# First attention of a four-layer kernel: mask pattern through TensorE, opening in another order, a fourth o_t, early residual loads, shared last norms

## The chip, the cores and the metric

The kernel runs on one core of a Trainium2 chip. A core has TensorE (PE, with its weight loads listed as PEld), VectorE (DVE), ScalarE (ACT), GpSimd (POOL) and SyncE (SP), and 16 DMA engines that SP, ACT and POOL feed from queues of their own. Each engine executes its instructions in order, and an instruction that waits holds those behind it. The metric is the device time of one execution in microseconds; the time before is the median of three runs. Times inside an execution count from the start of the profiled span. "L402" is line 402 of the kernel before.

## The reference, cut to what matters

The input x has 2048 rows of 576 columns. Four layers follow each other, each with a residual: attention (A), gated MLP (B), A, B.

```python
def A(x):                                   # 32 heads of 18
    q, k, v = split(x @ wqkv)
    idx = pos[:, None] - 2 * arange(8)      # 8 keys, two rows apart
    logits = where(idx >= 0, q . k[idx] * 18 ** -0.5, -1e9)
    return (softmax(logits) . v[idx]) @ wo
def B(x):
    z = gelu(x @ w_in)                      # 576 -> 4608
    z1, z2 = z[:, :2304], layernorm(z[:, 2304:])
    return (z1 * (w_sp @ z2 + b_sp)) @ w_out
x = x + A(layernorm(x)); x = x + B(layernorm(x)); x = x + A(layernorm(x)); x = x + B(layernorm(x))
```

## The kernel before, in words

The rows are held with even rows first and odd rows behind (`rows_of`), so that the eight keys of a row are neighbours. `layer_A` works on 17 query tiles of 120 rows (the first 128) with 128 keys each; a step is half a tile, that is 16 heads, so there are 34 steps (`NST`). An attention has an opening, the steps, and a tail.

**Row norms of the first layer.** `S_` takes the statistics of a row tile on DVE, `R_` the inverse root (an addition on DVE, a power on POOL), `A_` writes the normalised tile to one of four buffers `xn_bufs` on DVE. Tiles 0 to 3 are transposed into `xnT` by PE (`T_pe`, ScalarE copies), tiles 4 to 15 by DMA transposes on SP (`T_`, L266). The x tiles come in DMAs of one to four tiles. Before the norms PE runs 46 warm-up products of the identity (L626), and DVE fills unused weight rows with zeros (`zero_right`).

**Projections.** `VW(t, hh, dve)` makes half of v for tile t (five matmuls, `pv`) and evicts it into `v_ext` on DVE or ScalarE (L402, L404). `PG(d, qk, cc, dve)` makes 128 columns (block d of 0 to 4) of q or k for 512 rows (`pp`), evicts them into a staging tile `stg`, and when the staging tile has all its parts it issues DMAs that move each head to its place in `QK` (32 partitions a head; L78 on the queues it is given). Staging tiles are three of 1024 columns and, in the first layer, two pieces lent from the place of the gMLP weights `win2a`. (d, first half) for d of 3 and 4, and (4, each block of the second half), use the lent ones.

**The mask.** A head takes 18 of the 32 partitions that it has in `QK`. The 14 others hold a periodic pattern, so that the logits' matmul itself adds a large negative number outside the window. `build_window_rows` builds one period on POOL and DVE in `R`, writes it to DRAM (`win_period`, three DMAs on POOL's queue) and `load_pat` reads it back into the 14 rows of each quarter of `pat` (four DMAs on SP). `fill_window_rows(QK, half)` then copies the pattern over half of `QK` on DVE (L198); as it writes all partitions, the moves of q and k must come after it.

**Order of the opening.** All engines' orders are those of the program text (`manual_schedule`). After tiles 4 to 7 the text loads the pattern, normalises 8 to 11, fills half 0 of `QK`, takes the statistics of 12 to 15, and issues the PGs of columns 0 to 1023 in `order`, with R_ and A_ of 12 to 15 after the sixth entry and their transposes on SP after the last. Then come the v of tiles 4 to 7 (each first half evicted on DVE) and the first six PGs of the second half (`pre`, the first four evicted on DVE), with the first logits after two of them and the fill of half 1 after four.

**The steps.** Each step issues the logits of the next step (`L_mm`, L473), their exponentials on ScalarE (L482), and `PV`: 16 products with v (`O_ps`, L496), a reciprocal (L502), and the scaled result into `o_t` on DVE (L504). o_t buffers go round three; a full one is transposed by DMA on SP into `oT`, a ring of six tiles of 128 rows, directly (L511) or through `o_slot` (L515) and a DVE copy (`O_CP`, L524). The dictionary `table` then adds work by step number with `at(s, f, ...)`: the remaining PGs in steps 0 to 11 in the order of the list `pgs`, v, the output product `WO` (`pw`, L557) with its addition of the residual `xo` (L560), the load `XO` of two residual tiles at a time into three buffers, the store `XST`, and the next layer's row norm: `LN_STATS`, then `LN_AGGR` and `LN_POW` inside the next `PV`, then `LN_XN` on POOL (L259). `XN_ST` and `LN_T` store normalised rows to DRAM and read them back transposed for the gMLP.

**The tail.** Row tiles 12 to 15 (`tail_rows`) are normalised after the last step: two tiles' statistics, their roots, their POOL norms, then the same for the other two. `layer_B` begins with groups of eight units (`p1_group`, L907) whose results ScalarE evicts into row buffers `zp` (three); DVE and POOL normalise a finished row into `Z` (L971 to L980), which frees its buffer.

Of the kernel before, what the change touches and what calls it, by code (L numbers as in the profile page):

```python
# [63 lines left out]
class K:  # L64
# [50 lines left out]
    def build_window_rows(self, c, R):  # L115

# [5 lines left out]
        n = c.tile([P, 3], i32, name="win_n")  # L126
        g = c.tile([P, 3], i32, name="win_g")
        bits = c.tile([P, 5, 3], i32, name="win_bits")
        vf = c.tile([P, 5, 3], f32, name="win_vf")
        uu = c.tile([P, 4, 2], f32, name="win_uu")  # L130
        R0 = c.tile([P, 2, MR, 8], bf16, name="win_first")
        half = WB / 2
        nc.gpsimd.iota(n[:], pattern=[[1, 3]], base=15, channel_multiplier=1)
        nc.gpsimd.memset(R[:, 0, 0:8], half)
        nc.gpsimd.affine_select(out=R[:, 0, 0:8], in_=R[:, 0, 0:8], compare_op=ALU.is_ge, fill=-half,
                                base=0, pattern=[[1, 8], [0, 2], [-1, 8]], channel_multiplier=0)
        nc.gpsimd.memset(R[:, 1, 0:8], 0.0)
        nc.gpsimd.affine_select(out=R[:, 1, 0:8], in_=R[:, 1, 0:8], compare_op=ALU.not_equal, fill=-1.0,
                                base=-1, pattern=[[-1, 8], [0, 2], [1, 8]], channel_multiplier=0)
        nc.gpsimd.memset(R[:, 1, 7, :, 0:1], 1.0)  # L140
        for a, v in ((0, half), (1, 1.0)):
            nc.gpsimd.memset(R[:, a, 12, 0, :], v)
            nc.gpsimd.memset(R[:, a, 12, 1, :], -v)
        nc.gpsimd.memset(R[:, 0, 13], -2.5 * WB)
        nc.gpsimd.memset(R[:, 1, 13], 1.0)
        one = self.dram.tile([2, MR, 2 * P + 8], bf16, name="win_period")
        for xb in self.xn_bufs:
            nc.gpsimd.memset(xb[:, D:640], 0.0)

        def part0():  # L150
            nc.vector.tensor_scalar(out=n[:], in0=n[:], scalar1=15, scalar2=None, op0=ALU.bitwise_and)
            nc.vector.tensor_scalar(out=g[:], in0=n[:], scalar1=1, scalar2=None, op0=ALU.logical_shift_right)
            nc.vector.tensor_tensor(out=g[:], in0=g[:], in1=n[:], op=ALU.bitwise_xor)
            for i in range(4):
                nc.vector.tensor_scalar(out=bits[:, i, :], in0=g[:], scalar1=i, scalar2=1,
                                        op0=ALU.logical_shift_right, op1=ALU.bitwise_and)
            nc.vector.tensor_scalar(out=bits[:, 4, :], in0=n[:], scalar1=1, scalar2=None, op0=ALU.bitwise_and)

        def pads():
            nc.gpsimd.memset(pat[:], 0.0)  # L160

        def part1(eng):
            nc.vector.tensor_scalar(out=vf[:], in0=bits[:], scalar1=-2.0, scalar2=1.0, op0=ALU.mult, op1=ALU.add)
            Rf = R[:].rearrange("p a r b m -> p a r (b m)")
            nc.vector.tensor_scalar_mul(out=Rf[:, :, 0:8, :], in0=Rf[:, :, 0:8, :], scalar1=vf[:, 4, 1:2])
            nc.vector.tensor_tensor(out=uu[:], in0=vf[:, 0:4, 0:2], in1=vf[:, 0:4, 1:3], op=ALU.add)
            nc.vector.tensor_scalar_mul(out=Rf[:, 0, 8:12, :], in0=vf[:, 0:4, 1:2].to_broadcast([P, 4, 16]), scalar1=half)
            nc.vector.tensor_scalar_mul(out=Rf[:, 1, 8:12, :], in0=uu[:, :, 1:2].to_broadcast([P, 4, 16]), scalar1=0.5)
            for b_ in range(2):
                nc.vector.tensor_scalar_mul(out=R[:, 1, 8:12, b_, 0:1], in0=uu[:, :, 0:1], scalar1=0.5)  # L170
            for b_ in range(2):
                self.dma(one[:, :, b_ * P:(b_ + 1) * P].rearrange("a r (p m) -> p (a r) m", m=8),
                         R[0:16, :, :, b_, :].rearrange("p a r m -> p (a r) m"), eng=eng)

        def part2(eng):
            nc.gpsimd.tensor_copy(out=R0[0:1], in_=R[0:1, :, :, 0, :])
            nc.gpsimd.tensor_copy(out=R0[0:1, 1, 8:12, 0:1], in_=R[0:1, 1, 8:12, 0, 1:2])
            nc.gpsimd.memset(R0[0:1, 0, 11, :], 1.5 * WB)
            nc.gpsimd.memset(R0[0:1, 0, 13, :], -3.5 * WB)
            self.dma(one[:, :, 2 * P:2 * P + 8].rearrange("a r m -> (a r) m")[None, :, :], R0[0:1].rearrange("p a r m -> p (a r) m"), eng=eng)  # L180

        def load(eng):
            for j in range(4):
                self.dma(pat[32 * j + DH:32 * j + 32, :, :], one[:].rearrange("a r x -> r a x"), eng=eng)
        self.load_pat = load
        return part0, pads, part1, part2
# [42 lines left out]
    def ln_stats(self, pool, x_t, nrows, want_nmr=True, eps_eng=None):  # L229
        nc = self.nc  # L230
        eps_eng = eps_eng or nc.vector
        st = pool.tile([P, 2, nc.vector.BN_STATS_DIM], f32, name="ln_st", tag="ln_st", bufs=3)
        for s in range(2):
            nc.vector.bn_stats(out=st[:nrows, s, :], in_=x_t[:nrows, s * 288:(s + 1) * 288])
        mv = pool.tile([P, 2], f32, name="ln_mv", tag="ln_mv", bufs=3)
        nc.vector.bn_aggr(out=mv[:nrows, :], in_=st[:nrows, :, :])
        rstd = pool.tile([P, 1], f32, name="ln_rstd", tag="ln_rstd", bufs=3)
# [979 lines left out]
```

## Time and profile before

| what | value |
|---|---|
| median of 3 runs | 1168.77 us (1164.8 to 1170.26) |
| the profiled execution's own time | 1172.01 us |
| its span | 1170.2 us |
| PE, DVE, ACT, POOL busy | 98%, 47%, 29%, 24% of the span |
| first attention, to the first gMLP matmul | 126.39 us |
| first steps: output product of step 0 | 51.08 us |
| last step's output product | 120.64 us |
| mean granted TensorE clock | 0.997 |

A line of a timeline has the start, the duration of a group of like instructions, engine, line, operation, the output and input names, shapes and count; in brackets the idle time of the engine just before, and what ended it. A line of the chain of waits has start, duration, engine or DMA, name, line. A line of the windows has the stretch, its length, then for PE, PEld, DVE, ACT and POOL the busy time and number of instructions, then the granted PE clock (1.00 is full), the DMA engines' busy share and GB/s. Matmul ends are modelled and overlap by some 0.15 us.

### The profile page before, as it was taken

To read this page: it belongs to the slowest core of one execution; us is meant where nothing else is said; L and a number is where in the kernel's file an instruction comes from. 1 tells how busy PE (TensorE), PEld (TensorE's weight loads), DVE (VectorE), ACT (ScalarE), POOL (GpSimd) and SP (SyncE) were. 2 spreads that over 40 slices of the span, in tenths; PEclk is the share of its full clock that TensorE was granted. 3 is DMA by queue.
4 is the path that set the end of the run, shared out by engine and by line. 5 is a ranking of instruction groups with operands and counts; after the bars stand their busy time and mean duration, and the time that the engine had idled before them with its cause. 6 is when DMAs were issued, how large, how long until landed. Compare 5 with 4: busy or idle time off the path is not lost.

```text
span 1170.2 us, 19968 instructions
## 1 busy us (share of the span) xinstructions
PE 1150.5 (98%) x8163; PEld 612.5 (52%) x8258; DVE 550.0 (47%) x1167; ACT 338.8 (29%) x493; POOL 278.8 (24%) x389
## 2 busy tenths in 40 slices
PE   9999999999999999999999999999999999999998
PEld 5457544444444444457755774444444444444677
DVE  8668598322333332244555886963322223322321
ACT  5589455111100111101247884541011110111000
POOL 4659865000000000001153786640000000000000
PEclk9999999999999999999999999999999999999999
DMA  9599697000000000049646997930000000001332
GB/s 217 119 160 294 193 212 142 23 12 12 12 1 12 12 12 1 6 138 296 169 107 105 204 256 182 242 91 1 12 12 12 12 12 1 12 1 46 111 105 74
DMA packets 183240, 106.45 MB, mean 91 GB/s; under 512 B 135225, under 2 KB 164441, under 8 KB 183149
## 3 DMA queue, kind: packets, MB, share of 16 engines
q1 hardware_dynamic: 170285, 84.85, 31.6%
q0 software_dynamic: 6512, 14.57, 4.8%
q10 hardware_dynamic: 6352, 5.75, 1.6%
q8 instruction: 64, 1.05, 0.4%
q14 instruction: 27, 0.22, 0.1%
HBM read 42.40 MB, written 21.77 MB: 55 GB/s over the span
## 4 chain that ended last, share of the span: by engine, by line
PE 85%; POOL 7%; DMA 3%; DVE 2%; issue 2%; ACT 0%; SPq 0%; POOLq 0%; DVEq 0%; ACTq 0%
PE pg L1055 42%; PE po L1104 12%; PE pz L1031 6%; PE pz1s L1031 6%; PE pzs L907 5%; PE pp L436 4%; PE pz L907 4%; POOL ln_xn L259 4%; PE pv L410 2%; PE O_ps L496 1%; PE pw L557 1%; PE L_ps L473 1%; POOL ln_rstd L582 1%; DMA QK<-stg 1%; DMA o_slot<-o_t 1%
## 5 line engine op out<-in xcount | busy, mean ns | idle before, releaser
L1055 PE MATMUL pg<-Wq,Z 128*128 128x512 bf16 x2260 | 497.9, 379 | 2.5
L1055 PEld LDWEIGHTS <-Z 128*128 128x128 bf16 x2304 | 225.5, 98 | 271.8
L1059 DVE TENSOR_TENSOR g_tmp<-pg,ln_xn 128x512 f32<-128x512 f32 x144 | 99.6, 692 | 421.5 <-PE pg L1055 419.5
L1050 ACT ACTIVATE z1T<-pz 128x1024 bf16<-128x1024 f32 x36 | 34.9, 1021 | 500.8 <-PE pz L1031 500.8
L78 POOL DMA_DIRECT2D wout<-in_B_w_out_dram x4 | 4.3, 1070 | 598.8 <-PE pg L1055 598.8
L1104 PE MATMUL po<-wout,Z 128*128 128x288 bf16 x1152 | 141.4, 286 | 0.0
L482 ACT ACTIVATE P_sb<-L_ps 128x1440 bf16<-128x1440 f32 (+3 forms) x136 | 125.1, 972 | 21.1 <-PE L_ps L473 19.7
L1104 PEld LDWEIGHTS <-Z 128*128 128x128 bf16 x1152 | 112.7, 98 | 28.8
L907 PEld LDWEIGHTS <-xnT 128*128 128x128 bf16 (+1 forms) x800 | 68.7, 98 | 80.0 <-issue 15.5
L1060 DVE TENSOR_TENSOR Z<-g_tmp,z1T 128x512 bf16<-128x512 f32 x144 | 99.7, 692 | 12.2
L956 DVE BATCH_NORM_STATS2 z_st<-zp 128x6 f32<-128x512 bf16 (+1 forms) x160 | 91.0, 617 | 5.1 <-ACT zp L954 4.8
L1031 PEld LDWEIGHTS <-w 128*128 128x128 bf16 (+1 forms) x640 | 53.7, 97 | 74.0 <-issue 13.6
L436 PE MATMUL pp<-xnT,wqk_sb 128*128 128x512 bf16 x341 | 82.2, 382 | 2.5 <-DVE o_t L504 1.3
L259 POOL TENSOR_SCALAR ln_xn<-x_new,ln_mv,ln_rstd 128x576 bf16<-128x576 f32 x32 | 73.3, 2291 | 2.6
L1114 DVE TENSOR_TENSOR x_new<-po,xo 128x288 f32<-128x288 f32 (+1 forms) x64 | 28.8, 455 | 87.4 <-PE po L1104 83.9
L1031 PE MATMUL pz<-xnT,w 128*128 128x512 bf16 (+1 forms) x316 | 66.3, 380 | 0.2
L1031 PE MATMUL pz1s<-xnT,w 128*128 128x512 bf16 (+1 forms) x310 | 64.9, 379 | 0.9 <-issue 0.8
L78 POOL DMA_DIRECT2D QK<-stg x81 | 49.5, 614 | 46.0 <-DVE oT L524 14.8
L907 PE MATMUL pzs<-win2a,xnT 128*128 128x512 bf16 (+1 forms) x235 | 59.9, 364 | 0.4 <-issue 0.3
L907 PE MATMUL pz<-win2a,xnT 128*128 128x512 bf16 (+1 forms) x233 | 58.3, 357 | 0.6 <-issue 0.2
L980 POOL TENSOR_SCALAR Z<-zp,z_mv,z_rstd 128x256 bf16<-128x256 bf16 x32 | 55.7, 1740 | 3.4
L436 PEld LDWEIGHTS <-wqk_sb 128*128 128x128 bf16 x360 | 33.5, 98 | 38.3 <-DVE o_t L504 1.5
(113 smaller groups left out, 936.6 us busy)
## 6 DMA issues: line engine op xcount, KB each, us to landing
xres<-x_new SPq DMA_DIRECT2D x48, 288.0 KB
xo<-xres SPq DMA_DIRECT2D x32, 288.0 KB
wout<-in_B_w_out_dram POOLq DMA_DIRECT2D x4, 1296.0 KB, 8.2
xn_rows<-ln_xn SPq DMA_DIRECT2D x32, 160.0 KB
w<-in_B_w_in_dram SPq DMA_DIRECT2D x16, 256.0 KB
QK<-stg POOLq DMA_DIRECT2D x55, 72.0 KB, 5.2
xo<-xres SPq DMA_DIRECT2D x6, 576.0 KB
QK<-stg SPq DMA_DIRECT2D x39, 72.0 KB
```

The costliest lines, as they stand in the source:

```text
L78: return eng.dma_start(out=out, in_=in_)
L259: e.tensor_scalar(out=xn[:nrows, 0:D], in0=x_t[:nrows, :], scalar1=mv[:nrows, 0:1], scalar2=rstd[:nrows, 0:1], op0=ALU.subtract, op1=ALU.mult)
L436: nc.tensor.matmul(pp[:, :], lhsT=w, rhs=self.xnT[:, c, cc * 512:(cc + 1) * 512], start=(c == 0), stop=(c == 4))
L482: nc.scalar.activation(out=P_bufs[2 * jp + s % 2][:nk, :, :, 0:nq], in_=Lv[:nk, :, :, 0:nq], func=ACT.Exp, scale=scale)
L907: nc.tensor.matmul(out[:, o0:o0 + n], lhsT=self.xnT[r0:r1, c, r * P:(r + 1) * P], rhs=win2(c)[r0:r1, w0:w0 + n], start=start, stop=stop, t ...
L956: nc.vector.bn_stats(out=st[:, x // 512, :], in_=zp[:, x:x + min(512, w0 + n - x)])
L980: eng.tensor_scalar(out=Z[:, b0:b1, i, :], in0=zv[:, b0:b1, :], scalar1=mv[:, 0:1], scalar2=rstd[:, 0:1], op0=ALU.subtract, op1=ALU.mult)
L1031: nc.tensor.matmul(outs[a_], lhsT=w1[r0:r1, c, sub * P:(sub + 1) * P], rhs=self.xnT[r0:r1, c, q * 512:(q + 1) * 512], start=start, stop=st ...
L1055: nc.tensor.matmul(pg[:, :], lhsT=Z[:, jj, i, sub * P:(sub + 1) * P], rhs=Wq[q][:, i, :], start=(i == 0), stop=(i == NS - 1))
L1059: nc.vector.tensor_tensor(out=tmp[:], in0=pg[:, :], in1=bsp[:, qs], op=ALU.add)
L1060: nc.vector.tensor_tensor(out=uT(jj)[:, sub, qs], in0=tmp[:], in1=z1Ts[jj, sub][:, qs], op=ALU.mult)
L1104: nc.tensor.matmul(acc[hh], lhsT=u_rows(j, i), rhs=wouts[j // NJH][:, j % NJH, hh * 288:(hh + 1) * 288], start=(j == 0), stop=(j == NJ - 1))
```

## The change

- **Pattern.** `build_window_rows` writes the pattern transposed: rows of the period on the partitions, the 14 values of each head on the columns of a scratch tile `Wb` (768 columns per partition, lying in `oT`), three row blocks for each of the two sides. `part0` zeroes `Wb` and computes the bits on DVE, `part1` and `part2` write the values on POOL, `part3` transposes six 128x128 blocks on PE and copies them into `pat` on ScalarE. The DRAM round trip and its seven DMAs go.
- **Opening.** `part0` stands ahead of the identity and the zero fill of `wv`; the other zero fills move to POOL (`zero_more`), with `setup_bufs`, behind the third and fourth inverse roots. The statistics of the first tiles are cut in two parts (`S1`, `S2`), roots of tiles 2 and 3 are taken one by one. The fill of half 0 stands behind tiles 6 and 7; the norms of 8 to 11 and their transposes move between the PGs (after entry 4), those of 12 to 15 after entry 6. The PGs of the opening move heads on POOL, SP and ACT queues in a cycle of six (three POOL, two SP, one ACT). v of tiles 4 to 7 is evicted by ScalarE alone; `pre` uses DVE for two PGs, then comes the fill of half 1.
- **Steps.** (3, second half) is staged and moved in two blocks of 512 columns in a lent piece; the list of PGs begins with (4, 2), (3, 2), (0, 3); the load of w_o moves from step 0 to step 4. There are four o_t and, in the first layer, six residual buffers, so that the loads of the first six pairs are issued in steps 0 to 2. `O_CP` comes after the other work of its step.
- **Tail, both attentions.** The four last row norms share one `LN_REST`; the norms go from 15 down to 12, 15 and 14 on DVE, 13 and 12 on POOL. The small rings ln_st, ln_mv, ln_rstd have four buffers.

```diff
+        W = Wb.rearrange("p a b j q -> p a (b j) q")[:, :, :, DH:32]
         def part0():
+            nc.vector.memset(Wb[:], 0.0)
+            nc.gpsimd.iota(n[:, 0:3], pattern=[[8, 3]], base=127, channel_multiplier=1)
...
+        def part2():
+            e = nc.gpsimd
+            par = vf[:, 4, 3:4]
+            e.tensor_scalar(out=hh[:, 1, :], in0=hh[:, 0, :], scalar1=0.0, scalar2=WB, op0=ALU.is_ge, op1=ALU.mult)
+            e.tensor_scalar(out=W[:, 0, :, 0:8], in0=hh[:, 1:2, :].to_broadcast([P, 12, 8]), scalar1=-half, scalar2=par,
+                            op0=ALU.add, op1=ALU.mult)
...
+            e.tensor_scalar(out=W[:, 0, :, 8:12], in0=vf[:, None, 0:4, 3].to_broadcast([P, 12, 4]), scalar1=half, scalar2=None,
+                            op0=ALU.mult)
+            e.tensor_tensor(out=uu[:], in0=vf[:, 0:4, 0], in1=vf[:, 0:4, 1], op=ALU.add)
...
+        def part3():
+            pt = self.PT_tile([P, 6, P], bf16, "pt")
+            for k_ in range(6):
+                nc.tensor.transpose(pt[:, k_, :], Wb[:, k_ // 3, k_ % 3].rearrange("p j q -> p (j q)"), self.ident[:])
+            nc.scalar.copy(out=pat[:], in_=pt[:].rearrange("p (a b) x -> p a (b x)", a=2)[:, :, 0:2 * P + 8])
...
+    def zero_more(self, eng):
+        eng.memset(self.right["wqk4"][64:128, :], 0.0)
+        eng.memset(self.right["wo"][64:128, 4, :], 0.0)
...
-        o_bufs = [main.tile([P, 640], bf16, name=f"o_t{k_}") for k_ in range(3)]
+        o_bufs = [main.tile([P, 640], bf16, name=f"o_t{k_}") for k_ in range(4)]
...
-            alone = bool(lent) and d == 4 and cb == 1
+            alone = bool(lent) and d >= 3 and cb == 1
...
-                return p % 3
+                return p % 6
...
-            tails[i]["xn"] = self.ln_xn(tails[i]["x"], P, mv, rstd, nmr, eng="pool")
+            tails[i]["xn"] = self.ln_xn(tails[i]["x"], P, mv, rstd, nmr, eng="dve" if i >= NS - 2 else "pool")
...
+            rows[0]()
+            self.make_ident()
+            rows[1]()
             self.zero_right()
...
+            rows[2]()
             nc.scalar.copy(out=v_ext[:, :, :, DH:DH + 1], in_=self.ones[:, None, None, :].to_broadcast([P, NT, H, 1]))
+            rows[3]()
...
             S_(0)
             R_(0, 1)
-            S_(1)
+            S1(1)
+            A_(0)
+            S2(1)
             R_(1, 1)
-            A_(0)
             T_pe(0)
...
-                    PG(d, qk, cc, False, (nc.gpsimd, nc.sync) if d in (0, 4) else q2)
+                    PG(d, qk, cc, False, (nc.gpsimd, nc.sync, nc.gpsimd, nc.scalar, nc.gpsimd, nc.sync))
...
+                if k_ == 4:
+                    R_(8, 4)
+                    S_(12)
+                    A_(8, 9, 10, 11)
+                    T_(8, 9, 10, 11)
+                    S_(13, 14, 15)
+                if k_ == 6:
                     R_(12, 4)
                     A_(12, 13, 14, 15)
...
-                VW(t, hh, li == 0 and hh == 0)
+                VW(t, hh, False)
...
-            pgs.insert(0, pgs.pop(-2))
+            pgs = pgs[-2:-1] + pgs[6:8] + pgs[0:6] + pgs[8:10] + pgs[-1:]
...
-                at(max([s - 7] + [wo_steps[j][1] + 1 for j in last]), XO, i)
+                at(max([i // 4 if li == 0 and i < 12 else s - 7] + [wo_steps[j][1] + 1 for j in last]), XO, i)
...
-        for k_ in range(0, len(tail_rows), 2):
-            for i in tail_rows[k_:k_ + 2]:
-                at(NST + 3, LN_STATS, i)
-            at(NST + 3, LN_REST)
-            for i in tail_rows[k_:k_ + 2]:
-                at(NST + 3, LN_XN, i)
+        for i in tail_rows:
+            at(NST + 3, LN_STATS, i)
+        at(NST + 3, LN_REST)
+        for i in tail_rows[::-1]:
+            at(NST + 3, LN_XN, i)
...
-            PG(d, qk, cc, li > 0 or k_ < 4, q2)
-            if li == 0 and k_ == 3:
+            PG(d, qk, cc, li > 0 or k_ < 2, q2)
+            if li == 0 and k_ == 1:
                 self.fill_window_rows(QK, 1)
```

## Prediction

> **What bounds the kernel now.** I read the page's shares first. The median of the runs shown is 1168.77 us; the profiled execution took 1172.01 us, span 1170.2 us and 1.8 us around it. The sum is made against that execution and the difference is then taken off the median.
>
> ```profile
> PE 1150.5 (98%) x8163; PEld 612.5 (52%) x8258; DVE 550.0 (47%) x1167; ACT 338.8 (29%) x493; POOL 278.8 (24%) x389
> ```
>
> TensorE (PE) sets the time and no matmul of the layers goes away. What can be won is time in which PE waits or runs at a lower clock, so I read PE's timeline over the first attention (0 to 126.4 us) and both hand-overs into the gMLP, for idle times in brackets.
>
> ```profile
> 39.00 2.72 PE L410 MATMUL pv<-wv_sb,xnT 128*128 128x288 bf16 x15 [2.47 <-DVE v_ext L402]
> ...
> 69.69 1.25 PE L436 MATMUL pp<-xnT,wqk_sb 128*128 128x512 bf16 x5 [0.74 <-DVE o_t L504]
> ...
> 74.28 1.25 PE L436 MATMUL pp<-xnT,wqk_sb 128*128 128x512 bf16 x5 [0.60 <-DVE o_t L504]
> ...
> 84.83 0.55 PE L473 MATMUL L_ps<-QK 32*128 32x120 bf16 x3 [0.43 <-DMA QK<-stg]
> ...
> 147.94 1.37 PE L907 MATMUL pzs<-win2b,xnT 64*128 64x512 bf16 x5 [0.97 <-ACT zp L954]
> ...
> 723.50 1.37 PE L907 MATMUL pzs<-win2b,xnT 64*128 64x512 bf16 x5 [0.52 <-ACT zp L954]
> ```
>
> The reader is to see that the losses are few and that each has a name. The chain of waits in order of time says where the longest comes from:
>
> ```profile
> 14.31 6.51 DMA win_period<-win_first
> ...
> 22.23 2.93 DMA win_pat<-win_period
> 25.28 4.63 DVE QK L198 x4
> ...
> 36.06 1.04 POOL lnx_rstd L647
> 37.13 1.45 DVE ln_xn L654 x4
> 38.58 0.38 DVE v_ext L402
> 39.00 2.72 PE pv L410 x15
> ```
>
> The mask pattern travels to DRAM and back, the fill of QK starts only at 25.28, the moves into QK queue behind it on POOL, the inverse root for tiles 12 to 15 queues behind nine of those moves, DVE waits for it in A_, and the v eviction behind A_ holds PE. Last I read the windows with the granted clock:
>
> ```profile
> 36.71:40.12 3.41, 1.12 (x10) 0.89 (x10) 2.54 (x7) 0.31 (x1) 3.41 (x7) 1.00 0.67 167
> 40.12:43.54 3.42, 3.20 (x12) 1.62 (x11) 0.46 (x1) 0.49 (x2) 3.42 (x6) 0.50 0.77 175
> 145.92:149.33 3.41, 2.20 (x15) 0.80 (x14) 3.38 (x7) 1.82 (x4) 2.15 (x3) 1.00 0.71 139
> 149.33:152.74 3.41, 3.41 (x9) 1.23 (x10) 3.38 (x8) 1.72 (x3) 2.30 (x4) 0.50 0.52 114
> ...
> 5.99:9.40 3.41, 2.45 (x27) 1.84 (x25) 3.27 (x15) 1.71 (x3) 1.17 (x2) 1.00 1.04 338
> ```
>
> After a window of 3.4 us in which PE worked 1.12 or 2.20 us, the next 3.4 us have clock 0.50; after 2.45 us of work it stays 1.00. A stall of some 1.2 us can so cost up to 1.7 us more.
>
> **Mask pattern and opening (a cost).** DVE: three memsets (0.54, 0.30, 0.30) and eight small integer steps (2.28 to 3.98) stand before the first row statistics now. Afterwards one memset of 128x768 bf16 (0.4, between those of 0.30 and 0.54), eleven small steps at 0.21 each (2.3) and one memset (0.30): statistics start at 4.1 instead of 3.98, the inputs of POOL's part are ready at 3.85. POOL then writes the pattern: three steps of 8 columns and one add at 0.25 (scale row: 128x1, 0.23), one step of 4 at 0.22, two of 96 elements and two of 48. Per element POOL takes 3.6 ns (ln_xn, 576 in 2.29) to 6.1 (Z, 256 in 1.74, less 0.2 to start); 288 elements are 1.0 to 1.8 plus four starts of 0.2. With four memsets (0.2) and some 0.3 between dependent steps it is 3.3 to 4.3, taken 3.7: end at 7.55. POOL's first inverse root (0.6) now stands behind it, so A_(0) is at 8.35 instead of 5.96 and the first transposes of xn at 8.8 instead of 6.43. From there tile by tile (inverse root 0.65, A_ 0.35, transposes 0.45, v 0.61 each) the first q,k projection starts at 15.2 instead of 12.65: **-2.5** (between -1 and -4). The six pattern transposes (0.09 each) and ScalarE's copy (0.7) lie in this gap. The two zero fills and the setup memsets go behind the fourth inverse root on POOL (1.1, 0.6, 0.8); the zeros are there at 14.3, before the projection.
>
> In 5.99 to 9.40 PE would then work about 1.6 us (rest of the warm-up 0.64, six transposes 0.54, five 0.45): below 2.20, so clock 0.50 after it. With some 2.6 us of work there: **-1.3** (0 to -3.4). The Trainium skill (TensorE: Matmul & The Clock Gate, Part 1: The HAM clock gate) lets the clock fall after at least one idle window of about 3.4 us. By that rule none of these gaps would do it and this term is 0, a rival below; the trace, with 2.20 us of work in a halved case, speaks for the shorter one.
>
> **Stall at 39 (a gain).** The pattern is in SBUF by 9 us, the fill runs at 19.4 to 24.3 behind A_(6,7), the first moves are due at 29, one d at a time. The v evictions of tiles 4 to 7 leave DVE for ScalarE (0.40 each beside 0.61 of PE), so DVE's wait holds nothing. The stretch 36.5 to 44.84 loses 2.47 idle, and by the rows 0.87 (15 matmuls in 2.72 instead of 1.85), 0.2, 0.2 and 0.74 (8 in 2.47 instead of 1.73): **+4.4**. What is late next is SP. Its four transposes of tiles 8 to 11 wait for an inverse root behind four of d=0's moves on POOL (4x0.55, then 1.0) and hold SP for 5.3; the moves of d=1 to 4 (0.86 each) stand behind them. Counted from the end of the projection of (d=0, second block), the first logits come after 15.76; the last move they need is issued at 11.4 and lands 3.7 later (median of POOL's moves in 25 to 50 us; SP's are not shown), at 15.1. That fits by 0.7; with loaded landings of 6.9 (POOL, 50 to 90 us) it is 2.5 late. I take **-0.5** (0 to -3, with the clock). The seven moves on ScalarE's queue are not shown; at 0.42 (its load of x) to 0.86 (SP) they are at most 1.7 in a row against five PSUM buffers of 0.61 and more: 0.
>
> **The steps.** Free steps go by 1.915 us with projections and 2.06 with v and output. From 51.08 to 120.64 some are longer: 2.80 and 2.67 (o_t waits for its buffer's transpose), 2.59, 3.36 (logits wait for the moves of d=3), 2.50. Over the free ones this is 0.89, 0.75, 0.54, 1.3, 0.44: **+3.9** (2 to 3.9). A fourth o_t gives a transposition two steps (3.8 us) more, where DVE waited 1.26, 1.71 and 1.45. d=3's moves come in halves, the first at steps 1 and 2 instead of 10. That adds eight moves (POOL some 37 at 0.6 in 14 steps of 1.9: fits). x loads for six pairs move to steps 0 to 2, 1.7 MB onto queues at share 0.7 to 1.7, behind the four transposes of tiles 12 to 15 on SP. These land at 24.8 on the clock above and are needed at step 3, 27.8. The w_o load at step 4 is needed at step 13.
>
> **Shared norms.** Today POOL normalises row tiles 0 to 11 without a pause from 85.67, because moves held it until 85.07, and 12 to 15 until 144.7; z's first norm ends at 147.5, 21.1 us after the gMLP's first matmul at 126.39. Afterwards tile 0 starts 3 us earlier against that matmul; 12 to 15 have statistics at +4.1 (four pairs of 0.77 after the adds), four inverse roots until +6.9, two POOL norms of 2.55 until +12, z's root and norm until +14.6. Two norms on DVE cost 0.4 (bf16 row) to 0.8 (two f32 adds of 0.40), taken 0.6, and end before z's first aggregate. PE stalled at +20.6, so 5 us are spare. First hand-over: group 134.38 to 142.38 takes 8.0, the next 11.59: **+3.6** (2.4 to 3.6). Second: z ends at 719.5 instead of 723.04; its group takes 9.44 instead of 8.0: **+1.4** (0.5 to 1.4). The later copies into oT, larger rings and the reversed roots cost nothing by themselves: DVE is behind PE in each step.
>
> **Sum.** -2.5 -1.3 +4.4 -0.5 +3.9 +3.6 +1.4 = +9.0. The profiled execution would take 1163.0, the median 1159.8.
>
> **Rivals.**
> 1. *The opening costs more*: POOL's steps at the upper price and two windows at half clock, -4 and -3.4. For it: DVE, POOL and PE take turns there with nothing beside them. Gain 9.0-1.5-2.1 = 5.4: 1163.4.
> 2. *The moves stay late*: SP's blocked moves land at the loaded 6.9 and the logits stall and lose a window. Term -3 to -4.5 instead of -0.5. Against: share 0.7 in that stretch. Gain about 5.5: 1163.3.
> 3. *The clock holds*: the pauses fall on both sides of a window's edge, so that no window has under 2.45 us of work. No -1.3, gain 10.3, 1158.5. For it: the edges (40.12 and 149.33 are 32 times 3.41 apart) need not lie the same way in every execution. The Trainium skill's rule (the page and part named above) gives the same result.
> 4. *Slower*: the transposes of tiles 12 to 15 meet the early x loads. o_slot's transpose took 7.66 us at 66.01 (share 1.7). If four land one after the other at that price, the last is there at 18.2+30.6 = 48.8 instead of 27.8: PE waits 21 us at step 3 and a halved window costs 1.7, so 22.7 less 9.0 is 13.7 lost: 1182.5. It decides where PE waits over 7.3 us there, from some 4.2 us per transpose. Against: today's four, issued 1.31 apart at 43.72, hold no matmul.
> 5. *It doesn't do what it says*: the fill is still late since it stands behind A_(6,7). Then +4.4 goes: 1164.2. Against: five us spare.
>
> **Chances.** Forecast 0.58, clock holds 0.10, dearer opening 0.10, late moves 0.08, fill late 0.04, slower 0.10. A measurement of this kernel can tell about 0.5% (5.8 us) from no change. Late moves and a dearer opening fall short of that, the forecast's lower edge too for a part: faster 0.64, same 0.25, slower 0.11. The bounds of the terms reach from a loss of 1.1 to a gain of 12.3 and the runs of before scatter by about 2 us around a middle; leaving out the slower case and the worst corner of all terms at once, the range is a gain of 0.8 to 14.3: 1154.5 to 1168.
>
> **What would show it.** Right: first q,k projection at 16.5 (between 13.6 and 19); fill over by 25; no idle PE before the v of tiles 4 to 7; first logits near 44.7; steps without waits on o_t; last step at 116.7, gMLP from 122.4, its groups all 8.0, DVE doing two ln_xn of 0.6. Wrong: the projection as early as before or after 19; a clock of 0.50 past 20 us; PE waiting for xnT or QK in the steps; z's first norm over 19 us after the first gMLP matmul.

## The result and the profile after

The changed kernel takes 1175.8 us (median of 6 runs, 1172.15 to 1177.91), the kernel before in the same comparison 1167.82 (6 runs): ratio 1.0068, 95% interval 1.0044 to 1.0091. It is slower by 0.7%, 8 us, where 9 us of gain were forecast. The profiled execution after took 1177.02 us, span 1175.2; before, 1172.01 and 1170.2, so this pair of profiles shows 5.0 of the 8 us. In after.py lines lie elsewhere: v is evicted at L403 on ScalarE, `pv` is L409, `pp` L435, the logits L472, `o_t` L503, the copy of o_slot L523, x_new L559, the norm L256, the gMLP L924.

PE's page row first: it has as much work as before and waits longer.

```profile
PE 1150.6 (98%) x8169; PEld 611.8 (52%) x8264; DVE 551.2 (47%) x1166; ACT 341.8 (29%) x500; POOL 271.1 (23%) x389
```

PE's timeline of the changed kernel, the lines with the first projection and the longest waits of the first attention, and the first gMLP matmul (start, us, engine, line, in brackets the idle time before and what ended it):

```profile
14.29 8.80 PE L435 MATMUL pp<-xnT,wqk_sb 128*128 128x512 bf16 x39
...
43.43 3.76 PE L409 MATMUL pv<-wv_sb,xnT 128*128 128x288 bf16 x15 [4.98 <-ACT v_ext L403]
...
84.83 1.38 PE L409 MATMUL pv<-wv_sb,xnT 128*128 128x288 bf16 x5 [4.53 <-DVE o_t L503]
...
135.32 0.59 PE L924 MATMUL pz<-win2a,xnT 128*128 128x512 bf16 x2
```

The stall of 2.47 at 39 that was to go is there, at the same v of tiles 4 to 7, with twice the length and another releaser, ScalarE. A second one of 4.53 stands in the steps. Milestones from PE's timelines, before and after: first projection 12.65 and 14.29; first logits 44.77 and 50.38; output product of step 0 51.08 and 56.69; last step 120.64 and 129.58; first gMLP matmul 126.39 and 135.32; start of the gMLP's fourth group 153.97 and 159.30. So 1.6 us are lost before the projections, 4.0 until the first logits, 3.3 in the steps, and 3.6 come back in the gMLP.

ScalarE's timeline names the first stall (ACTq lines are issues of DMAs):

```profile
41.33 1.61 ACTq L78 DMA_DIRECT2D QK<-win2a  x2
42.98 1.61 ACT L403 CAST v_ext<-pv 128x288 bf16<-128x288 f32 x5 [6.10 <-DMA QK<-win2a]
```

and the chain of waits what ScalarE waited for:

```profile
32.99 8.26 DMA QK<-stg
41.33 0.80 ACTq L78
...
42.98 0.41 ACT v_ext L403
43.43 3.76 PE pv L409 x15
```

In the compiled program the DMAs of SP and ScalarE take eight completion semaphores in turn, and each waits until the eighth before it has landed. The trace's instruction records show it: the DMAs that SP and ScalarE issue in the opening name semaphores 100, 102 and 104 to 109 one after the other, POOL's name 111 to 118, and at 41.27 ScalarE waits for semaphore 104. That is the one of its own move of d=2, issued at 32.99 and landed 8.26 later. So ScalarE's first move of d=4 waits for that landing, and the evictions of v stand behind it. The second stall in the same view:

```profile
74.55 9.21 DMA o_slot<-o_t
...
83.78 0.35 DVE oT L523
...
84.32 0.47 DVE o_t L503
...
84.83 1.38 PE pv L409 x5
```

The first o_slot is transposed late and lands late, and its copy into oT, an item of step 10, holds DVE for 5.48 us (o_slot was issued 14.9 us after the first output product before, 17.9 after). Both stalls cost clock too; windows of the changed kernel, PE's busy time behind the stretch's length, granted clock, DMA share and GB/s last:

```profile
39.41:42.82 3.41, 0.00 (x0) 0.00 (x0) 0.77 (x2) 0.00 (x0) 1.82 (x4) 0.95 1.28 134
...
45.70:49.15 3.45, 3.23 (x12) 1.50 (x11) 0.43 (x1) 0.80 (x2) 0.00 (x0) 0.50 0.62 133
...
84.10:87.50 3.40, 2.67 (x39) 1.62 (x40) 2.52 (x8) 0.67 (x1) 1.64 (x4) 0.50 1.08 136
```

### The profile page after: what moved, and what is told of

Same layout as the page of the kernel before. It is cut to its first block, busy times and chain, and to the rows that moved or that the text cites. A ratio compares the mean times of both kernels' runs of the same rounds, so it can differ in the third digit from the quotient of the medians.

```text
span 1175.2 us, 19942 instructions
## 1 busy us (share of the span) xinstructions
PE 1150.6 (98%) x8169; PEld 611.8 (52%) x8264; DVE 551.2 (47%) x1166; ACT 341.8 (29%) x500; POOL 271.1 (23%) x389
## 4 chain that ended last, share of the span: by engine, by line
PE 93%; DMA 2%; DVE 2%; POOL 1%; issue 1%; ACT 1%; ACTq 0%; DVEq 0%; POOLq 0%; SPq 0%
PE pg L1072 42%; PE po L1121 12%; PE pz L924 6%; PE pz L1048 6%; PE pz1s L1048 6%; PE pzs L924 6%; PE pp L435 6%; PE pw L556 3%; PE pv L409 3%; PE O_ps L495 2%; PE L_ps L472 1%; DMA o_slot<-o_t 1%; DMA QK<-stg 1%; POOL ln_xn L256 1%; ACTq L78 0%
## 5 line engine op out<-in xcount | busy, mean ns | idle before, releaser
L924 PEld LDWEIGHTS <-xnT 128*128 128x128 bf16 (+1 forms) x800 | 68.3, 97 | 75.8 <-issue 10.4
L435 PE MATMUL pp<-xnT,wqk_sb 128*128 128x512 bf16 x341 | 82.3, 382 | 1.3 <-issue 0.2
L256 POOL TENSOR_SCALAR ln_xn<-x_new,ln_mv,ln_rstd 128x576 bf16<-128x576 f32 x28 | 64.1, 2290 | 3.2 <-DMA xn_rows<-ln_xn 0.6
L409 PE MATMUL pv<-wv_sb,xnT 128*128 128x288 bf16 x340 | 51.9, 294 | 9.6 <-ACT v_ext L403 5.0
L924 PE MATMUL pz<-win2a,xnT 128*128 128x512 bf16 (+1 forms) x233 | 58.3, 357 | 0.9 <-DVE x_new L559 0.5
L924 PE MATMUL pzs<-win2a,xnT 128*128 128x512 bf16 (+1 forms) x235 | 58.6, 358 | 0.4 <-issue 0.3
L971 ACT ACTIVATE zp<-pz 128x1024 bf16<-128x1024 f32 (+2 forms) x56 | 36.6, 720 | 63.3 <-PE pz L924 63.3
```

Of the source, the lines that this page charges most:

```text
L256: e.tensor_scalar(out=xn[:nrows, 0:D], in0=x_t[:nrows, :], scalar1=mv[:nrows, 0:1], scalar2=rstd[:nrows, 0:1], op0=ALU.subtract, op1=ALU.mult)
L409: nc.tensor.matmul(pv[:nk, 0:288], lhsT=self.xnT[:, c, k0_(t):k0_(t) + nk], rhs=wv_sb[:, c, hh * 288:(hh + 1) * 288], start=(c == 0), stop ...
L435: nc.tensor.matmul(pp[:, :], lhsT=w, rhs=self.xnT[:, c, cc * 512:(cc + 1) * 512], start=(c == 0), stop=(c == 4))
L924: nc.tensor.matmul(out[:, o0:o0 + n], lhsT=self.xnT[r0:r1, c, r * P:(r + 1) * P], rhs=win2(c)[r0:r1, w0:w0 + n], start=start, stop=stop, t ...
```

## The experiments

The theory at the start: moves on ScalarE make the first stall, early residual loads the second; the rest of the change is worth what the prediction said. Ratios below are to the kernel before in the same comparison, and differences between kernels are taken from these ratios unless the text says otherwise; 0.001 is 1.17 us.

| kernel | median us | ratio, 95% interval |
|---|---|---|
| the change | 1175.8 | 1.0068, 1.0044 to 1.0091 |
| e1: d=4's moves off ScalarE | 1178.19 | 1.0107, 1.009 to 1.0124 |
| e2: norms of 8 to 11 put back | 1173.41 | 1.0066, 1.0049 to 1.0082 |
| e9: no moves on ScalarE | 1176.5 | 1.0069, 1.0044 to 1.0095 |
| e6: e2 and e9 together | 1170.33 | 1.0037, 1.0021 to 1.0053 |
| e3: late residual loads | 1174.93 | 1.0083, 1.0065 to 1.01 |
| e5: late copy of o_slot | 1184.65 | 1.0156, 1.0133 to 1.0179 |
| e10: e6, w_o at step 0 | 1174.03 | 1.0056, 1.0037 to 1.0075 |
| e7: e10, late residual loads | 1167.69 | 1.0019, 1.0006 to 1.0032 |
| e12: e7, old order of the moves | 1164.58 | 0.9977, 0.9965 to 0.999 |
| e13: e12, pattern behind four roots | 1167.36 | 1.0007, 0.9996 to 1.0018 |
| e4: before, new last norms | 1162.74 | 0.9981, 0.9967 to 0.9996 |
| e8: e4, fourth o_t | 1164.48 | 0.9995, 0.9975 to 1.0015 |
| e14: e4, early residual loads | 1173.59 | 1.0068, 1.0049 to 1.0086 |
| e15: e14, fourth o_t | 1171.82 | 1.0042, 1.0026 to 1.0059 |
| e11: e4, v of 4 to 7 on ScalarE | 1162.39 | 0.9963, 0.9945 to 0.9982 |

**The opening: e1, e2, e9, e6.**

```diff
-PG(d, qk, cc, False, (nc.gpsimd, nc.sync, nc.gpsimd, nc.scalar, nc.gpsimd, nc.sync))
+PG(d, qk, cc, False, (nc.gpsimd, nc.sync, nc.gpsimd, nc.scalar if d < 4 else nc.gpsimd, nc.gpsimd, nc.sync))   # e1
+PG(d, qk, cc, False, (nc.gpsimd, nc.sync) if d in (0, 4) else q2)                                              # e9, e6
...
+R_(8, 4); S_(12); A_(8, 9, 10, 11); T_(8, 9, 10, 11)    # e2, e6: ahead of the fill
 self.fill_window_rows(QK, 0)
```

> The changed kernel, with the two moves of d=4 that went on ScalarE's queue in the opening put on POOL's queue; ScalarE keeps its five moves of d=0 to 3. Theory H (held queue): in the changed kernel ScalarE sits at the first of these two from 36.9 to 41.33 us, because a move of d=2 of its own lands only 8.3 us after its issue, and the v evictions stand behind it. Then PE's idle 4.98 us before the v of tiles 4 to 7 is gone (under 0.5), the first logits come at 42 to 44 us instead of 50.4, the next logits may wait up to 2 us for late moves, and the time falls by 5 to 8 us against the changed kernel: about the time of before. Rival L (load): all moves are late because transposes and moves load the DMA engines, whoever issues them; then PE waits for QK at the first two logits instead, the output product of step 0 stays within 2 us of 56.7, and the time falls by less than 2 us.

Half of it held: the stall at v is gone, but one of 5.62 stands at 46.62, at the next projections, which read tiles 8 to 11, and the step-0 output product comes at 57.83. The second stall (3.67) ends at 85.11, as late as in the change (84.83). The chain of waits of e1:

```profile
28.38 2.38 POOL QK L78 x4
...
30.78 1.05 POOL lnx_rstd L646
...
31.85 0.46 DVE ln_xn L653 x2
32.31 14.18 DMA xnT<-ln_xn x2
...
46.62 0.58 PE pp L435
```

The transposes waited for the norms, and these for POOL's inverse root, which stands behind four moves on POOL. SP issues the four between 32.31 and 39.74, and the last lands at 46.49.

> The changed kernel, with the norms and the four SP transposes of tiles 8 to 11 put back ahead of the fill of QK, so that SP has them behind it when the moves begin; ScalarE keeps all seven moves. Theory H with its cause (the transposes between the moves make SP's and ScalarE's moves late): SP is free for the moves from 29 us, ScalarE's wait at d=4 shrinks under 1.5 us, PE's idle before the v of tiles 4 to 7 is under 1 us, first logits at 42 to 45 us, time 5 to 8 us below the changed kernel. Rival: ScalarE's own issues of 0.8 us each are what costs, wherever the transposes stand; then the idle stays over 3 us and the time within 2 us of the changed kernel.

First logits at 46.19 instead of 50.38, the wait on ScalarE cut from 4.98 to 1.62 and 1.18, the step-0 output product at 52.51; a second stall of 2.67 remains at 78.78, and the time is not told apart from the change's.

> The changed kernel with the opening's moves on POOL and SyncE alone, as in the kernel before; the norms and transposes of tiles 8 to 11 stay behind five projections. It fills the fourth field of a table: changed kernel 1175.8, norms alone put back 1173.4, both put back 1170.3. If ScalarE's moves and the late norms each cost by themselves, it is 3 us under the changed kernel, 1172.7. Rival, after the run with only d=4's moves taken off ScalarE (1178.2, with the transposes of tiles 8 to 15 late on SyncE): the moves then stand ahead of those transposes on SyncE, PE waits for xnT, and the time is 1176 or more; ScalarE's moves are then only bad together with norms in their old place.

The time is the rival's, its reason holds only in part. PE does wait 3.05 for xnT at 43.76, but the first logits come at 46.01 and the step-0 output product at 53.02, 3.7 us earlier than in the change. That is lost again in the steps: o_slot is issued at 72.41, just behind the load of w_o, which held SP for 2.71, and lands 11.26 later; the second stall is 8.06 and ends at 84.74, where that of the change ends at 84.83.

> The changed kernel, with the opening's moves on POOL and SyncE alone, queue by queue as in the kernel before, and the norms and transposes of tiles 8 to 11 ahead of the fill of QK again. The pattern by TensorE, the early fill, the v evictions on ScalarE and the late half of the attention stay. If the first stall is ScalarE held at its own DMA issues together with norms that come too late for SyncE, it goes whole: v of tiles 4 to 7 without idle PE of over 1 us, first logits at 42 to 44 (50.4 in the changed kernel, 46.2 with the norms alone moved), time about 1169. Rival: the early fill and the moves collide whoever issues them (the moves' landing rose from 3.7 to 6.7 us); then the wait turns up at a transpose or a move, first logits stay past 47, and the time at 1173 or more.

No wait at v, first logits at 42.08, but the step-0 output product only at 50.01, where QK's last moves land, and the second stall (2.33) remains: 3.6 us gained of the 7 expected. Neither half does it alone: with late transposes the wait turns up at xnT (e9), with moves on ScalarE it stays at v (e2).

One thing in these kernels is not as the expectations of e6, e7 and e13 have it. The norms of 8 to 11 now stand ahead of the fill on DVE, and the fill of half 0 starts at 24.02 in e6, 24.97 in e7, 24.46 in e12 and 26.52 in e13, against 18.38 in the change and 25.28 before. So early norms and an early fill are one choice, the gain of e6 is had with a fill that is late again, and the early fill was never run with the rest in order.

The DMA view shows the opening's moves in the landing times (72 KB each, count, median us from issue to landing, stretch 25 to 50 us), first of the changed kernel, then of e6:

```profile
QK<-stg POOLq DMA_DIRECT2D x9, 72.0 KB, 5.4
...
QK<-win2a POOLq DMA_DIRECT2D x3, 72.0 KB, 8.4
```

```profile
QK<-stg POOLq DMA_DIRECT2D x11, 72.0 KB, 4.3
QK<-win2a POOLq DMA_DIRECT2D x4, 72.0 KB, 3.1
```

Before it was 3.7 and 3.9. The Trainium skill (DMA: Bandwidth & Descriptors, Issuing engines are not separate DMA queues) says that DMAs of ScalarE, SyncE and GpSimd share 16 DMA engines, and that a further issuing engine saves only the time of issuing. The rows fit that: with a third queue, and the transposes late on SP, the landings became longer, not shorter, and ScalarE itself was held. Either one alone leaves them longer too: 5.4 and 5.7 in e9, which has only the late transposes, 5.4 and 5.0 in e2, which has only the third queue.

**The steps: e3, e5, e10, e7.**

```diff
-at(max([i // 4 if li == 0 and i < 12 else s - 7] + ...), XO, i)
+at(max([s - 7] + ...), XO, i)                      # e3, e7
-ocps.append((min(2 * t + 6, s), t))
+ocps.append((s, t))                                # e5
-at(4, self.load_wo, nc.sync)
+at(0, self.load_wo, nc.sync)                       # e10, e7
```

> The changed kernel, with the residual loads at the steps of the kernel before (steps 6, 8, 12 and so on instead of 0 to 2), six buffers kept. The opening should stay as in the changed kernel (v idle of about 5 us). Theory X (early loads): the six loads take 3.7 us of SP's issue time ahead of the first o_slot transpose and 1.7 MB of the DMA engines' time, so it is issued at 74.55 and lands at 83.76, and DVE's copy into oT, and behind it PE, wait 4.5 us and lose about 2.9 us more at half clock. Then the transpose is issued 3 to 5 us earlier, PE's stall at step 13 falls under 1.5 us and the time falls by 4 to 7 us. Rival W: the eight added moves of d=3, or the w_o load moved to step 4 (1.4 us on SP just ahead of that transpose), make it late: then the stall stays above 3 us and the time falls by less than 2.5 us.

The stall shrinks from 4.53 to 0.64, as theory X had it, but the next o_slot (issued 79.92, landed 8.96 later) makes one of 2.68 at 89.97, and the first stall (3.49) stays. No gain that can be told.

> The changed kernel, with the copy of a landed o_slot into oT asked for one step before the output projection that reads it, instead of at step 2t+6 (so the copy of t=2 no longer stands at step 10 on VectorE). If the second stall (4.5 us at 84.8, and some 2.9 us of half clock behind it) is the copy's place in VectorE's order, it goes: no idle PE over 1 us between 75 and 95, time about 1169 (6 to 7 us under the changed kernel's 1175.8). Rival: the transposed rows are late for their reader too, since SyncE issues them 17.9 us after step 0 and they land 9.2 us later; then the same wait only moves to the output projection, and the time stays at 1175 to 1176.

This edit does not isolate its point: the copy now stands behind the transpose of a later tile into the same slot, waits for that one too, and copies that tile's rows, so it computes something else. PE waits 8.82 for it at 95.89. Where a copy could stand later without this was not tried.

> The run with the opening's queues and norms put back (1170.3), with w_o loaded at step 0 instead of 4, and the residual loads early as in the changed kernel. If w_o, which stands directly ahead of the first o_slot on SyncE (1.4 us of issue), makes the stall near step 11, the stall of 2.3 us there is gone and the time is that of the run with both put back, 1167.7. Rival: the three x loads of the steps 0 to 2 do it (four issues of 0.5 to 0.9 us on SyncE, and their bytes): the stall stays over 1.5 us and the time at 1170.

Its place at step 4 is not what hurts: with it at step 0, in the middle of the early loads, o_slot is issued at 69.89 and lands 11.60 later, against 67.77 and 7.03 in e6. The time is 2.2 us longer by the ratios, but the intervals overlap.

> As the run with the opening's queues and norms restored, and also the residual loads seven steps ahead of their use and w_o at step 0, as in the kernel before. Left of the change: the pattern by TensorE and the early fill, v evictions on ScalarE, the order of the moves inside the steps, a fourth o_t, six residual buffers, the shared last norms. If both stalls are matters of what stands ahead on SyncE and ScalarE, it is at the time of the kernel before with the new tail alone, 1162.7, or up to 4 us below it (1158.5 to 1163). Rival: the order of the moves inside the steps (d=4 and halves of d=3 first) is what makes o_slot late; then a stall of 2 us or more stays between 70 and 95, and the time is 1166 or more.

It isolates the residual loads: against e10 nothing else is changed, and the time falls by 4.3 us, with intervals that lie apart. No wait over 0.40 is left between 51 and 118, and the steps take 66.33 from first to last output product (72.89 in the change). But at 118.78 PE waits 1.56 for o_t and at 128.66 1.09 for x_new: POOL's row norms have become the bound, and they start late.

**The order of the late moves and the pattern: e12, e13.**

```diff
-pgs = pgs[-2:-1] + pgs[6:8] + pgs[0:6] + pgs[8:10] + pgs[-1:]
+pgs.insert(0, pgs.pop(-2))        # e12, e13; d=3 in one move again, pre as before
...
+rows[2]()                         # e13: behind R_(3, 1); rows[3]() behind VW(2, 1)
```

> The run with queues, norms and loads put back (1167.7), and also the order and size of the late moves as in the kernel before (d=3 whole again, d=4 not first). In that run's profile POOL is still issuing moves until 81.1, each waiting for a landing, so its first row norm starts at 84.6 against 79.6 in the kernel before with the new norms, and POOL, at 3.9 us a row, sets the hand-over (x_new waits for ln_xn). If the order does that, POOL's first row norm comes 29 to 32 us after the first output product instead of 34.5, and the time falls by 2 to 4 us, to 1164 to 1165.5. Rival: the remaining 5 us against 1162.7 come from the opening alone (first projection 1.9 us later), and the time stays at 1167 or more.

It held, for three edits together: the order of the moves, d=3 in one move, and the place of `pre` and the fill of half 1. POOL's timeline in e7, then in e12, up to the first row norm:

```profile
78.69 0.51 POOL L78 DMA_DIRECT2D QK<-win2a  x1 [0.96 <-DMA QK<-win2a]
...
80.60 0.51 POOL L78 DMA_DIRECT2D QK<-win2a  x1 [0.42 <-DMA QK<-win2a]
83.33 0.57 POOL L78 DMA_DIRECT2D win2a<-in_B_w_in_dram  x1 [2.22 <-DMA QK<-win2a]
...
84.62 2.30 POOL L256 TENSOR_SCALAR ln_xn<-x_new,ln_mv,ln_rstd 128x576 bf16<-128x576 f32 x1
```

```profile
77.35 1.00 POOL L78 DMA_DIRECT2D QK<-win2a  x2 [0.97 <-DMA QK<-stg]
...
79.72 2.30 POOL L256 TENSOR_SCALAR ln_xn<-x_new,ln_mv,ln_rstd 128x576 bf16<-128x576 f32 x1
```

The last moves share the two lent pieces of win2a, the next weights go there too, and each issue on POOL waits for a landing; the row norms are queued behind. The first row norm starts at 84.62 in e7 and at 79.72 in e12, 30.1 us after the first output product, as expected; the twelfth starts at 125.47 and 120.92. POOL does not make up the late start. Which of the three edits did it, no run separates.

Put back one after the other, the three groups give 3.6 us (queues and norms, e6), 2.1 (loads and w_o, e6 to e7) and 4.9 (e7 to e12), together 10.6 us, which is the distance from the change to e12.

> The run with queues, norms, loads and the order of the moves put back (1164.6), with POOL's writes of the pattern behind the first four inverse roots, and TensorE's six transposes of it behind v of tile 2; the fill stays early. If the opening's cost is the 3.4 us that POOL spends ahead of the first root, the first projection comes at 12.4 to 13 instead of 14.3, with no half clock in the opening, and the time falls by 1 to 2 us, to 1162.5 to 1163.5. Rival: the transposes and ScalarE's copy of the pattern cost the same wherever they are, or the start of the projections isn't what sets the first output product (the moves land later): the first projection is earlier, and the time stays at 1164 to 1165.

Neither side: the projection comes at 13.72, but POOL's pattern, 3.7 us here (9.77 to 13.43), now stands ahead of the roots of tiles 4 to 7, PE waits 2.47 for xnT at 26.23, and the clock falls. 3.5 us slower than e12.

**Parts alone on the kernel before: e4, e8, e14, e15, e11.** Their diffs are those lines of the change, put into before.py: the last norms (all five), `range(4)` for o_bufs (e8, e15), `p % 6`, two more pieces in xo_bufs and the place of XO (e14, e15), `VW(t, hh, False)` (e11).

> The kernel before with only the tail of the change (four shared norms, 15 and 14 on DVE, rings of four, roots reversed), in both attentions. Theory: the term of the prediction is right by itself, 3.6 us at the first hand-over and up to 1.4 at the second, so 4 to 5 us below the kernel before. Rival: the stall at the first hand-over goes in the changed kernel only because the gMLP starts 9 us later there while POOL started its norms 7 us later; by itself it leaves 1 to 2 us of the stall, and the gain is 1 to 3 us.

Faster by 0.2% (2.2 us by the ratio, 3.1 by the medians).

> The kernel before with the shared last norms and a fourth o_t, nothing else. The prediction gave the freed waits on o_t (0.74 and 0.60 us in the profile of before) as part of a gain in the steps: 1 to 2 us under the 1162.7 of the kernel before with the new norms alone. Rival: with the copies of o_slot waiting on the same landing, a fourth o_t frees nothing, and the time is 1162.7 within 1 us.

The rival: no gain that can be told from none.

> The kernel before with the shared last norms (1162.7), and six residual buffers loaded at the steps 0 to 2, nothing else. If these loads, in a stretch in which the DMA engines are full from 55 to 90 us, make the first o_slot land late, a stall of 2 to 5 us stands at step 10 to 12, with half clock behind it, and the time is 1166 to 1169. Rival: they only hurt with o_slot already late from the opening or the moves' new order; then no such stall, and the time is 1162.7 within 1.

The loads alone cost 1.0068 against 0.9981 of e4, 10 us. PE's timeline of e14, then its chain:

```profile
64.16 1.25 PE L436 MATMUL pp<-xnT,wqk_sb 128*128 128x512 bf16 x5 [1.97 <-DVE o_t L504]
...
76.60 2.32 PE L436 MATMUL pp<-xnT,wqk_sb 128*128 128x512 bf16 x5 [5.21 <-DVE o_t L504]
```

```profile
55.47 8.08 DMA oT<-o_t
63.62 12.37 DMA oT<-o_t
```

The transposes that free o_t take 8.08 and 12.37 us to land; between the two waits shown a third of 1.85 stands at 70.83, for a staging tile (`stg`). POOL's 72 KB moves in the same stretch (50 to 75 us, DMA view) land after a median of 6.3 us in e4 and 9.9 in e14: the loads go onto DMA engines that are full in e4 already (share 1.0 to 1.3 from 55 to 90 us).

> The kernel before with the shared last norms, early residual loads and a fourth o_t. If the fourth o_t covers part of the late landings, the wait on o_t at 64 (2.0 us) goes, the one at 76 (5.2 us) shrinks or turns into a wait for the copy of o_slot, as in the changed kernel, and the time is 2 to 5 us under the 1173.6 with three: 1168.5 to 1171.5. Rival: the copy of o_slot holds VectorE as long as o_t did, so the fourth buffer covers nothing: 1172.5 to 1174.5.

The fourth buffer takes back some 3 us by the ratios, under 2 by the medians, and the intervals overlap, so the gain is not certain. The wait at 64 is gone; one of 5.16 stands at 71.64, where DVE waits 7.95 for a move of QK to free its staging tile.

> The kernel before with the shared last norms (1162.7) and all v evictions of tiles 4 to 7 on ScalarE. The opening of before had a stall of 2.5 us at v in its profile and none in that of the run with the new norms, with the same instructions there: if it comes and goes with the landing that VectorE waits for, ScalarE's eviction takes away the bad executions: median 1161 to 1162, and no execution above 1166. Rival: VectorE's wait is not what delays the first output product (moves of QK land later than v is ready): no difference, 1162.7 within 1.

Faster than both kernels, no wait at v in its profile; against e4 the intervals overlap, and one of eight executions took 1167.74. Whether it beats e4 stays open.

## Why the prediction was wrong, step by step

- **Stall at 39, +4.4: failed.** The step was "The v evictions of tiles 4 to 7 leave DVE for ScalarE ... so DVE's wait holds nothing", with ScalarE's seven moves priced "at most 1.7 in a row against five PSUM buffers of 0.61 and more: 0". An issue was priced by its own duration. ScalarE waited 6.10 us before one, for a landing of 8.26, v stood behind, and PE idled 4.98. Rival 2 was right that moves land late (it took 6.9; the medians were 5.4 and 8.4), but saw the wait at the logits and not at v. Nor was +4.4 there to win in full. With the hold gone (e6) the step-0 output product comes at 50.01, only 1.1 earlier than before, as QK's last moves land then. And the term was too large against the median: the same instructions gave 2.47 of idle PE there in the profile of before, 2.62 in e8, 1.00 in e15, 0.36 in e4, 0.34 in e14. The profiled execution of before (1172.01) was above all three runs shown; that the stall was part of why is likely, not shown.
- **Steps, +3.9: failed, by the rival's mechanism in another place.** Steps 0 to 11 of the change go without a wait on o_t, as forecast. Rival 4 saw the early x loads delay transposes, but those of tiles 12 to 15 at step 3, which took no harm; the transposes of o_t and o_slot were hit, and the loads' effect on those had been put at nothing without a reason. e14 gives the price on the kernel before, 10 us with three o_t; between e8 and e15, with four, 5.5. With the opening put back, taking the early loads away gives 4.3 (e10 to e7); in the change itself it gave nothing that can be told (e3).
- **d=3 in halves, "POOL some 37 at 0.6 in 14 steps of 1.9: fits": failed.** Again issues were counted without landings: in e7 POOL's issues wait for landings until 83.33, and its row norms start late. e7 to e12 is 4.9 us, for the halves, the order and the place of `pre` together.
- **Opening, -2.5 and -1.3: too dear, right in kind.** POOL wrote the pattern in 3.4 us (3.33 to 6.74; 3.7 taken), the first projection came 1.6 later, without half clock in the changed kernel. In e12, with the same opening, the half clock was there (first projection at 15.52), as in e3 (15.49). The early fill came as forecast (18.4 to 23.2 instead of 25.3 to 30.1). Whether it is worth anything stays open, as every kernel that puts the norms of 8 to 11 back loses it. What e12 (0.9977) against e4 (0.9981) does say is that the pattern by TensorE, v on ScalarE, the fourth o_t and the six residual buffers together bring nothing that can be told.
- **Shared norms, +3.6 and +1.4: the first right to 0.1 in the profile** (gMLP groups of 8.0, DVE's two norms 0.58 each), the second 0.84 against 1.4: from the gMLP's first matmul to its fourth group it takes 24.38 instead of 25.22. The group of 9.44 takes 7.99, but a new wait of 0.46 for x_new stands at 710.72. By itself (e4) 2.2, interval 0.5 to 3.8.

The clock behind the opening's gaps, in e12 and then in the changed kernel (windows of one microsecond, PE's busy time; clock, DMA share and GB/s last):

```profile
9.00:10.00 1.00, 0.76 (x8) 0.77 1.12 330
10.00:11.00 1.00, 1.00 (x6) 0.50 1.07 308
```

```profile
9.00:10.00 1.00, 0.76 (x9) 1.00 1.09 311
10.00:11.00 1.00, 1.00 (x10) 1.00 1.09 274
```

Ahead of it PE idled in the same two places (0.59 and 0.95 us), in the changed kernel for 0.58 at 6.86 as well, and the clock falls to 0.50 in e12, where PE idled less, and not there. By the rule that the prediction took from the Trainium skill (TensorE: Matmul & The Clock Gate, Part 1: The HAM clock gate), after an idle window of about 3.4 us, it should fall in neither; e12 and e3 speak against that as a necessary condition. The windows of before that the prediction shows speak against it more plainly, with 1.12 and 2.20 us of work in them and 0.50 behind. Between 6.56 and 9.53 PE ran only transposes in e12, and no run shows whether these count as work. That the window runs on its own, so that its phase differs from run to run, as the same section says, fits both. What sets the fall stays open.

Open is why the parts do not add up: on the changed kernel late loads alone gave nothing (e3), on e4 early loads alone cost 10 us. That one late landing can hide another is shown by e9, where 3.7 us won in the opening were gone when the second stall ended; that the same lies behind e3 is argued.

## What to carry to other kernels

An issue on an in-order engine costs its duration only while what it must wait for (a buffer, a completion semaphore shared with other queues) has landed; price the landing under the load of that stretch, and list what is queued behind on each issuing engine. Where the DMA engines are full, a load moved forward can delay the transfers that are needed first, as in e14. Before a stall is counted as a gain, see whether it is in the median: take a second profile, or the clock and span of other runs.

## What was not expected of the hardware

- Landing times of like DMAs differ two- to fourfold: 72 KB moves from 3.7 (before) to 8.4 us (the change) and 9.9 (e14) in the median, DMA transposes of one o_t up to 12.37 us in e14. In e8's profile, which has no added load, one takes 15.87 (o_slot at 72.34); that execution took 1172.85 where another of e8 took 1160.3.
- PE stood for 2.99 us in the middle of an output product at 75.14 in e10, waiting for nothing that the profile shows. The trace has one packet of 16 KB on the instruction queue from 69.82 that took 3.64 us, where others of that run took 0.92 to 1.56; that PE waited for instructions is likely, not shown.
